# Products with the values in plain float32, two heads side by side, in a fused attention and MLP kernel

## The chip, the cores and the metric

The kernel runs on one core of one Trainium2 chip. The metric is the device time of one execution in microseconds (us). Three runs of the kernel before took 716.34, 716.54 and 716.68 us; the median is 716.54.

TensorE (PE in the profile; PEld is its loading of weights) multiplies matrices: a stationary operand of up to 128 rows by 128 columns is loaded, and a moving operand of up to 512 columns streams past it into a bank of PSUM. VectorE (DVE), ScalarE (ACT) and GpSimd (POOL) work element by element, and SyncE (SP) issues the transfers.

## The reference

Attention with a window and sinks, then a two-layer MLP with squared ReLU:

```python
scores = (1 / sqrt(64)) * q @ k.T            # q, k, v: 4 batches, 8 heads, 768 positions, 64 wide
keep = (key < n_sink) | (0 <= query - key < window)      # n_sink 4, window 128
a = exp(scores_kept - max);  a = a / (sum(a) + 1e-9)
x = a @ v                                     # then (3072 tokens, 512)
g = s * relu(x @ w_in) ** 2 + b               # w_in 512 x 2048
out = g @ w_out                               # w_out 2048 x 512
```

All of it is float32.

## The kernel before, in words

The 3072 tokens are eight chunks of 384 (`CH`), three blocks of 128 (`BLK`, `P`). `ORDER` gives the batch and the half of the sequence of each chunk: chunks one and two are the first halves of batches 0 and 1, three and four their second halves, five and six the halves of batch 2, seven and eight those of batch 3. So of chunks three to eight, four are second halves and two are first halves.

The main loop at the end of the kernel (lines 785 to 800) runs the MLP of chunk c step by step (`moe_steps`: 16 first-layer steps `l1` with twelve matmuls of 384 columns at L610, 16 second-layer steps `l2` with nine of 512 columns at L630), and after each step it issues the slots of the attention of chunk c+1 that are due by then. So matmuls of the attention stand between blocks of MLP matmuls in TensorE's order, which is the order in which the code issues them.

Attention of the first two chunks is the class `Plain` (L461 to L566), with products in plain float32; its product with the values is L555: for each block of keys and each of a pair's two heads, a stationary block of values of 64 columns, with the first head's result in partitions 0 to 63 of a bank and the second's in 64 to 127. Attention from the third chunk on is `attn_slots` (L418), which the change touches. There most products are made in `float32r`, a form of float32 of which TensorE takes a reduced precision in one instruction; to keep the precision, an operand is split into a high part (a copy to float32r) and a low part (what the copy left out).

`attn_slots` has one unit for each head h and block i of 128 queries, so six for a pair of heads, and one slot for each unit. A slot t runs, in this order: loads and preparations that are due (`ahead`), the products with the values of unit t-7 (`unit_c`, `LC` = 7), the scores of unit t (`unit_a`), the work on the transposed exponentials of unit t-4 (`unit_b`, `LB` = 4), the ends of a pair (`sinks`, `scaled`), and the transpose of unit t-3 (`turn`).

- `load_pair` (L244) loads a pair's queries and values, five slots ahead of its first unit; `load_keys` a head's keys, through one buffer; `prep_head` (L278) splits a head's queries, keys and values. The values become a stationary block of 128 columns, high part in 64 of them and low part in the others (L293 ACT, L294 POOL).
- `unit_a` (L297): two matmuls (L308, L309) for scores, a mask with maximum (L313), the exponential (L319), and POOL's additions and sink copies (L322, L323).
- `turn` (L329): the exponentials of 128 queries and 128 keys (those of two key blocks laid over one another) are transposed on TensorE.
- `unit_b` (L331): the two key blocks are separated by a multiplication with the masks `split` (L342 DVE, 256 columns), and the result is split into a high part (L344 ACT) and a low part (L345 POOL) in the tile `hl`, one for each head. The very first block of a sequence has one key block alone (L347, L348).
- `unit_c` (L360): at a head's block i=1 and at its block i=2, the products with the values. At i=1 high and low parts against the block of keys cur-1 (256 columns each, L382), and in second halves against one further block (128 columns each). At i=2 both parts of the last 128 columns in one matmul of 2 x 128 (L374), and two of 256 columns (L382). Each product has the high values' result in one half of the bank and the low values' in the other; L389 (ACT), L390 (DVE) and L392 (POOL) add them.
- `sinks` and `scaled` add the sinks' values (L406, L407) and divide by the sums (L413, L414), and L415 and L416 split the result for the MLP.

The planner that orders the instructions keeps this order on each engine, and each engine works through its own queue in order.

Of the kernel before, what the change touches and what calls it, by code (L numbers as in the profile page):

```python
# [6 lines left out]
F32 = mybir.dt.float32  # L7
F32R = mybir.dt.float32r
# [19 lines left out]
MDT = mybir.dt.bfloat16  # L28
WUP = 256.0
LOADS = 8  # L30
SMB, HLB = 4, 2
WARM0 = 14
NARROW, NEARLY = 2, 8
RB, VB = 1, 2
E0 = 16
PART = 256
FN, FB, FC = (3, 2), (7, 8), (11, 12)
# [4 lines left out]
def tile_kernel(ctx, tc, qT, kT, k0, v, vsk, n_sink, window, w, s, b, out):  # L42
# [201 lines left out]
    def load_pair(k, pr):  # L244

        pp = Chunk()
        k.pairs[pr] = pp
        half = k.half
        nkb, k0, kw, v0 = 3 + half, (0, 2 * P + 2 * NS)[half], (3 * P + 2 * NS, 4 * P + 2 * NS)[half], half * 2
        pp.q = wk.tile([P, CH], F32, name="qraw", tag="qraw", bufs=1)  # L250
        nc.sync.dma_start(pp.q, qT[k.b, pr, :, half * CH:(half + 1) * CH])
        pp.v = wk.tile([P, 4, 2, D], F32, name="vraw", tag="vraw", bufs=1)
        nc.sync.dma_start(pp.v[:, :nkb], v[k.b, pr, :, v0:v0 + nkb])
        for hh in range(2):
            hd = Chunk()
            hd.nkb, hd.kw, hd.k0, hd.half = nkb, kw, k0, slice(hh * D, (hh + 1) * D)
            hd.q, hd.v = pp.q[hd.half], pp.v[:, :, hh]
            k.heads[2 * pr + hh] = hd
        pp.psk = psks[(k.c * (H // 4) + pr // 2) % 2]
        pp.zz = wk.tile([P, BLK, 2], F32, tag="zz", name="zz", bufs=2)  # L260

    def load_keys(k, h):

# [14 lines left out]
    def prep_head(k, h):  # L278
        hd = k.heads[h]
        kw = hd.kw  # L280
        hd.qs = wk.tile([P, CH], F32R, tag="qs", name="qs")

        other = slice(D, 2 * D) if h % 2 == 0 else slice(0, D)
        nc.scalar.copy(hd.qs[hd.half], hd.q)  # L284
        hd.kh = wk.tile([P, 4 * P + 2 * NS], F32R, tag="kh", name="kh")
        hd.kl = wk.tile([P, 4 * P + 2 * NS], F32R, tag="kl", name="kl")
        nc.scalar.copy(hd.kh[:, :kw], hd.k[:, :kw])  # L287
        nc.vector.tensor_tensor(out=hd.qs[other], in0=hd.q, in1=hd.qs[hd.half].bitcast(F32), op=ALU.subtract)  # L288
        nc.gpsimd.tensor_tensor(out=hd.kl[:, :kw], in0=hd.k[:, :kw], in1=hd.kh[:, :kw].bitcast(F32), op=ALU.subtract)  # L289
        hd.vv = wk.tile([P, 4, P], F32R, tag="vv", name="vv", bufs=VB)  # L290
        a, c = (0, D) if h % 2 == 0 else (D, 0)
        n = hd.nkb
        nc.scalar.copy(hd.vv[:, :n, a:a + D], hd.v[:, :n, :])  # L293
        nc.gpsimd.tensor_tensor(out=hd.vv[:, :n, c:c + D], in0=hd.v[:, :n, :], in1=hd.vv[:, :n, a:a + D].bitcast(F32),  # L294
                                op=ALU.subtract)

    def unit_a(k, h, i, sc):  # L297

# [31 lines left out]

    def unit_b(k, h, i, tp):  # L331

        sm, c0, p0, _ = k.cc.pop((h, i))
        hd = k.heads[h]
        if i == 0:
            hd.hl = wk.tile([P, 2, 2 * CH], F32R, name="hl", tag="hl", bufs=HLB)

        a, z = (P if p0 is None else 0), 2 * P
        hi, lo = (hd.hl[:, t, i * z + a:(i + 1) * z] for t in range(2))
        if p0 is not None:  # L340
            both = wk.tile([P, 2 * P], F32, tag="two", name="two", bufs=2)
            nc.vector.tensor_tensor(out=both.rearrange("p (s c) -> p s c", s=2), in0=tp.unsqueeze(1).to_broadcast([P, 2, P]), in1=split,  # L342
                                    op=ALU.mult)
            nc.scalar.copy(hi, both)  # L344
            nc.gpsimd.tensor_tensor(out=lo, in0=both, in1=hi.bitcast(F32), op=ALU.subtract)  # L345
        else:
            nc.scalar.copy(hi, tp)  # L347
            nc.vector.tensor_tensor(out=lo, in0=tp, in1=hi.bitcast(F32), op=ALU.subtract)  # L348
        pp = k.pairs[h // 2]
        if h % 2 == 1 and i == BLK - 1:  # L350
            z0 = 12 * NS + h // 2 % 2 * 4
            zr = wk.tile([P, 2, BLK, 2], F32, tag="zr", name="zr")
            zh = wk.tile([P, BLK, 2], F32R, tag="zh", name="zh")
            nc.vector.tensor_scalar(out=zr[:, 0], in0=pp.zz, scalar1=1e-9, scalar2=None, op0=ALU.add)
            nc.vector.reciprocal(out=zr[:, 1], in_=zr[:, 0])
            nc.vector.tensor_copy(zh, zr[:, 1])
            nc.gpsimd.tensor_copy(out=pp.psk[:, :, z0:z0 + 2], in_=zh.bitcast(F32))
            nc.vector.tensor_tensor(out=pp.psk[:, :, z0 + 2:z0 + 4], in0=zr[:, 1], in1=zh.bitcast(F32), op=ALU.subtract)

    def unit_c(k, h, i):  # L360

        hd = k.heads[h]
        pp = k.pairs[h // 2]
        cur = i if k.half == 0 else i + 1
        if i == 1:
            hd.o = ps("o")
            hd.n = 0

        mm = []
        if i == BLK - 1:
            c0 = (2 * i + 1) * P
            nc.tensor.matmul(hd.o[:, i * P:], hd.vv[:, cur, :], hd.hl[:, :, c0:c0 + P], start=False, stop=False)  # L374
        if i > 0:
            mm.append((cur - 1, 2 * i - 1, 2))
        if i == 1 and k.half == 1:
            mm.append((0, 0, 1))
        for kb, c0, n in mm:
            for t in range(2):  # L380
                q0 = c0 // 2 * P
                nc.tensor.matmul(hd.o[:, q0:q0 + n * P], hd.vv[:, kb, :], hd.hl[:, t, c0 * P:(c0 + n) * P],  # L382
                                 start=(hd.n == 0), stop=(i == BLK - 1 and kb == cur - 1 and t == 1))
                hd.n += 1
        if i == BLK - 1:
            a, c = (0, D) if h % 2 == 0 else (D, 0)
            if h % 2 == 0:
                pp.x = wk.tile([P, CH + P], F32, tag="y", name="y", bufs=3)
            nc.scalar.copy(pp.x[a:a + D], hd.o[c:c + D])  # L389
            nc.vector.tensor_tensor(out=pp.x[a:a + D], in0=hd.o[a:a + D], in1=pp.x[a:a + D], op=ALU.add)  # L390
            if h % 2 == 1:
                nc.gpsimd.tensor_tensor(out=pp.x[:, CH - P:CH], in0=pp.x[:, CH - P:CH], in1=pp.x[:, CH:], op=ALU.add)  # L392
                pp.x = pp.x[:, :CH]
            if h % 4 == 3:
                ts = ps("ts")
                for j in range(BLK):
                    nc.tensor.transpose(ts[:, j * P:(j + 1) * P], pp.psk[:, j, :], ident)  # L397
                pp.xs = k.pairs[h // 2 - 1].xs = wk.tile([P, CH], F32R, tag="xsk", name="xsk", bufs=1)
                nc.scalar.copy(pp.xs, ts[:, :CH])
                nc.vector.tensor_tensor(out=pp.xs[32:64], in0=ts[32:64, :CH], in1=pp.xs[32:64].bitcast(F32), op=ALU.subtract)  # L400
# [17 lines left out]
    def attn_slots(c):  # L418
        k = new_chunk(c)
        units, ahead = [], {}  # L420
        for pr in range(H // 2):
            h, t0 = 2 * pr, 2 * BLK * pr
            units += [(h + hh, i) for hh in range(2) for i in range(BLK)]
            todo = ((-5, load_pair, pr), (-5, load_keys, h), (11, load_sinks, pr), (-2, prep_head, h), (-2, load_keys, h + 1),
                    (1, prep_head, h + 1))
            for d, fn, a in todo:
                ahead.setdefault(max(t0 + d, 0), []).append((fn, a))
        n = len(units)
        ends = {}
        for pr in range(H // 2):  # L430
            t = 4 * BLK * (pr // 2 + 1) - 1 + LC
            for d, fn in zip((LD if pr < H // 2 - 2 else LDL)[pr % 2], (sinks, scaled)):
                ends.setdefault(t + d, []).append((fn, pr))

        def slot(t):
            def f():

                for fn, a in ahead.get(t, ()):
                    fn(k, a)
                if t == 0:  # L440
                    k.bank = ps("sc")
                if 0 <= t - LC < n:
                    unit_c(k, *units[t - LC])
                if t < n:
                    unit_a(k, *units[t], k.bank)
                if 0 <= t - LB < n:
                    unit_b(k, *units[t - LB], k.bank[:, 3 * P:])
                for fn, pr in ends.get(t, ()):
                    fn(k, pr)
                if t + 1 < n + LB:  # L450
                    k.bank = ps("sc")
                if 0 <= t + 1 - LB < n:
                    turn(k, *units[t + 1 - LB], k.bank[:, 3 * P:])
            return f

        parts = [slot(t) for t in range(n + LC + LDL[1][1])]
        parts.pop(n + LB)
        return k, parts
# [391 lines left out]
```

## Time and profile before

One execution was profiled: it took 715.33 us, and its span from the first to the last instruction is 713.6 us.

| engine | busy us | share of the span | instructions |
|---|---|---|---|
| PE (matmuls) | 693.0 | 97% | 3908 |
| PEld (weight loads) | 613.8 | 86% | 3908 |
| DVE | 500.6 | 70% | 1186 |
| ACT | 469.4 | 66% | 1153 |
| POOL | 385.3 | 54% | 671 |

The mean granted clock of TensorE is 0.998 of its full speed. The main groups are L610 (1536 matmuls, 297.6 us) and L630 (1152 matmuls, 295.9 us), the MLP.

How to read it: a matmul's row gives its start and its length, and lengths of neighbours overlap, since they are pipelined; the distance from one start to the next is what a matmul adds to the time. In a group's row, the number behind the bar is the busy time, then the mean length of one in ns, then the idle time of the engine before them and what ended it. Shapes such as 128\*64 are rows by columns of the stationary block. A row of the timeline with a count behind it merges neighbours that are alike.

### The profile page before, as it was taken

Reading aid. Unit: us, or ns where it says so; the run is one execution under the profiler, and the core shown is the slowest. Engines: PE = TensorE matmul, PEld = TensorE weight load, DVE = VectorE, ACT = ScalarE, POOL = GpSimd, SP = SyncE. Lnnn points to the kernel's source line nnn. Section 1 sums busy time; section 2 is a strip of 40 time slices with the busy share of each in tenths; the row PEclk is TensorE's granted clock in tenths of the full one; section 3 lists DMA queues with packets and bytes.
Section 4 is the critical chain, followed back from the end, with each engine's and each line's share of the span. In section 5 each row is a group of like instructions: output and inputs, shape, how many; then the busy total and the mean of one; then the engine's idle time right before and its main releaser. Section 6 shows DMA issues by size and latency. Waiting matters only on the chain.

```text
span 713.6 us, 12060 instructions
## 1 busy us (share of the span) xinstructions
PE 693.0 (97%) x3908; PEld 613.8 (86%) x3908; DVE 500.6 (70%) x1186; ACT 469.4 (66%) x1153; POOL 385.3 (54%) x671
## 2 busy tenths in 40 slices
PE   8799999999999999999999999999999999999996
PEld 4477877899989998899999999899998999899895
DVE  6899979488865798657885788657786588743321
ACT  6999975578845786467764787556774677733222
POOL 2356635379843899336671788625773488700000
PEclk9999999999999999999999999999999999999999
DMA  7873140322112122021111121111221221000001
GB/s 283 355 269 130 34 155 27 108 66 57 57 56 75 42 81 55 17 82 58 50 57 65 51 72 51 35 64 53 57 63 37 80 66 42 1 30 15 1 1 49
DMA packets 27382, 52.63 MB, mean 74 GB/s; under 512 B 3504, under 2 KB 15536, under 8 KB 25392
## 3 DMA queue, kind: packets, MB, share of 16 engines
q1 hardware_dynamic: 27312, 51.79, 22.0%
q8 instruction: 33, 0.54, 0.3%
q14 instruction: 37, 0.30, 0.1%
HBM read 45.49 MB, written 6.29 MB: 73 GB/s over the span
## 4 chain that ended last, share of the span: by engine, by line
PE 76%; DVE 6%; ACT 3%; POOL 2%; issue 1%; DMA 1%; POOLq 0%; ACTq 0%; DVEq 0%
PE h L610 32%; PE po L630 32%; PE o L382 3%; PE sc L308 2%; PE sc L309 2%; PE sc L329 2%; DVE w L230 1%; DMA w<-in_w 1%; DVE w L220 1%; PE o L374 1%; DVE wt L219 1%; POOL hl L345 1%; POOL kl L289 1%; PE os L406 1%; PE ts L397 1%
## 5 line engine op out<-in xcount | busy, mean ns | idle before, releaser
L610 PE MATMUL h<-x,w 128*128 128x384 f32 x1536 | 297.6, 342 | 6.0 <-DVE w L230 2.6
L630 PE MATMUL po<-w,g 128*128 128x512 f32 x1152 | 295.9, 402 | 0.0
L610 PEld LDWEIGHTS h<-x,w 128*128 128x128 f32 x1536 | 264.8, 188 | 14.3 <-DVE w L230 3.3
L630 PEld LDWEIGHTS po<-w,g 128*128 128x128 f32 x1152 | 209.8, 189 | 43.7 <-issue 1.6
L616 DVE SCALAR_TENSOR_TENSOR r<-h,sb,r 128x384 f32<-128x384 f32 x112 | 68.9, 615 | 78.8 <-ACT r L613 77.9
L613 ACT ACTIVATE r<-h 128x384 f32<-128x384 f32 x128 | 62.9, 491 | 90.6 <-PE h L610 81.1
L619 DVE SCALAR_TENSOR_TENSOR g<-r,sb,g 128x384 fp32r<-128x384 f32 x112 | 91.5, 817 | 31.3 <-ACT g L618 29.7
L345 POOL TENSOR_TENSOR hl<-two,hl 128x256 fp32r<-128x256 f32 x128 | 102.3, 801 | 15.4 <-ACT hl L344 13.3
L322 POOL TENSOR_TENSOR sm<-sm 128x128 f32<-128x128 f32 x128 | 67.4, 527 | 61.2 <-ACT sm L319 59.0
L319 ACT ACTIVATE sm<-sm,negm 128x264 f32<-128x264 f32 (+1 forms) x144 | 72.1, 500 | 28.5 <-DVE negm L313 27.3
L618 ACT ACTIVATE g<-r,sb 128x384 fp32r<-128x384 f32 x112 | 69.1, 617 | 22.7 <-DVE r L616 21.9
L206 POOL TENSOR_TENSOR w<-w 128x256 int32<-128x256 int32 x60 | 48.6, 840 | 54.3 <-DVE zf L532 15.1
L289 POOL TENSOR_TENSOR kl<-kraw,kh 128x528 fp32r<-128x528 f32 (+1 forms) x48 | 60.8, 1266 | 20.7 <-ACT kh L287 20.4
L344 ACT CAST hl<-two 128x256 fp32r<-128x256 f32 x128 | 50.5, 394 | 26.0 <-DVE two L342 25.7
L342 DVE TENSOR_TENSOR two<-sc,split 128x256 f32<-128x256 f32 x128 | 53.1, 417 | 5.8 <-POOL hl L345 5.5
L323 POOL COPY psk<-sm 128x24 f32<-128x24 f32 x144 | 35.5, 247 | 17.1 <-ACT sm L319 17.0
L382 PE MATMUL o<-hl,vv 128*128 128x256 f32 (+1 forms) x256 | 44.3, 275 | 0.0
L382 PEld LDWEIGHTS o<-hl,vv 128*128 128x128 f32 x256 | 39.6, 188 | 3.2
L288 DVE TENSOR_TENSOR qs<-qraw,qs 64x384 fp32r<-64x384 f32 x48 | 39.7, 827 | 3.5 <-ACT qs L284 1.9
L313 DVE CUSTOM_DVE_ANT_0 sm<-sc,msk 128x264 f32<-128x264 f32 (+1 forms) x80 | 32.0, 400 | 14.0 <-PE sc L309 13.4
L308 PE MATMUL sc<-kh,qs 128*128 128x264 f32 (+1 forms) x144 | 41.6, 291 | 0.0
L313 DVE CUSTOM_DVE_ANT_0 sm<-sc,m_all 128x264 f32<-128x264 f32 x64 | 27.3, 426 | 20.1 <-PE sc L309 18.4
(139 smaller groups left out, 924.0 us busy)
## 6 DMA issues: line engine op xcount, KB each, us to landing
w<-in_w SPq DMA_DIRECT2D x15, 1024.0 KB, 10.5
kraw<-in_kT SPq DMA_DIRECT2D x32, 264.0 KB, 2.6
out<-ot SPq DMA_DIRECT2D x24, 256.0 KB, 2.0
qraw<-in_qT SPq DMA_DIRECT2D x24, 192.0 KB, 2.4
vraw<-in_v SPq DMA_DIRECT2D x16, 256.0 KB, 2.7
kraw<-in_kT SPq DMA_DIRECT2D x16, 200.0 KB, 2.4
vsraw<-in_vsk SPq DMA_DIRECT2D x24, 64.0 KB, 2.1
vraw<-in_v SPq DMA_DIRECT2D x8, 192.0 KB, 2.4
```

Of the source, the lines that this page charges most:

```text
L289: nc.gpsimd.tensor_tensor(out=hd.kl[:, :kw], in0=hd.k[:, :kw], in1=hd.kh[:, :kw].bitcast(F32), op=ALU.subtract)
L313: nc.vector.tensor_tensor_reduce(out=sm[:, :n], in0=sc[:, :n], in1=m, scale=-0.125, scalar=BIG, op0=ALU.add, op1=ALU.min, accum_out=negm[: ...
L319: nc.scalar.activation(sm[:, :n], sm[:, :n], AF.Exp, bias=negm[:, uu], scale=-1.0, accum_out=pp.zz[:, i, hh:hh + 1])
L322: nc.gpsimd.tensor_tensor(out=sm[:, c1:c1 + P], in0=sm[:, p1:p1 + P], in1=sm[:, c1:c1 + P], op=ALU.add)
L345: nc.gpsimd.tensor_tensor(out=lo, in0=both, in1=hi.bitcast(F32), op=ALU.subtract)
L382: nc.tensor.matmul(hd.o[:, q0:q0 + n * P], hd.vv[:, kb, :], hd.hl[:, t, c0 * P:(c0 + n) * P], start=(hd.n == 0), stop=(i == BLK - 1 and kb ...
L610: nc.tensor.matmul(h[:, :CH], weight[f][:, 0, wi, cc * P:(cc + 1) * P], x[xi][:, cc, :], start=(i == 0), stop=(i == 11))
L613: nc.scalar.activation(r, h[:, :CH], AF.Relu, scale=1.0 / WUP)
L616: nc.vector.scalar_tensor_tensor(out=hr, in0=h[:, :CH], scalar=sw_ap, in1=r, op0=ALU.mult, op1=ALU.mult)
L618: nc.scalar.activation(gg[:, 0, :], hr, AF.Identity, bias=b_ap, scale=1.0)
L619: nc.vector.scalar_tensor_tensor(out=gg[:, 1, :], in0=hr, scalar=b_ap, in1=gg[:, 0, :].bitcast(F32), op0=ALU.add, op1=ALU.subtract)
L630: nc.tensor.matmul(po[tb], gg[:, gi, tsl], weight[f][:, 1, wi, :], start=(f == 0 and i == 0), stop=(f == NF - 1 and i == 2))
```

## The change

From the third chunk on the values stay as they are loaded, and are no longer split: `load_values` loads a pair's values into a tile of the ring `vv`, five slots behind the pair's first unit (`VL` = 5), not with the queries five slots ahead of it. The transposed exponentials stay whole as well: L342 writes them into a tile `pp.t` for the two heads of a pair (the ring `hl`, the same size), and L344, L345 and L348 go. The products of both heads are made at the units i=1 and i=2 of the pair's second head, in plain float32: stationary 64 columns of values, the first head's result in partitions 0 to 63 and the second's in 64 to 127, in one bank for the pair. So the sum of parts (L390, L392) goes, and one copy of 128 x 384 is left of L389.

```diff
-SMB, HLB = 4, 2
+SMB, HLB, VL = 4, 2, 5
...
-RB, VB = 1, 2
+RB = 1
...
 def load_pair(k, pr):
...
-        pp.v = wk.tile([P, 4, 2, D], F32, name="vraw", tag="vraw", bufs=1)
-        nc.sync.dma_start(pp.v[:, :nkb], v[k.b, pr, :, v0:v0 + nkb])
+        pp.v0, pp.nkb = v0, nkb
...
+    def load_values(k, pr):
+        pp = k.pairs[pr]
+        pp.v = wk.tile([P, 4, 2, D], F32, name="v", tag="vv", bufs=2)
+        nc.sync.dma_start(pp.v[:, :pp.nkb], v[k.b, pr, :, pp.v0:pp.v0 + pp.nkb])
...
 def prep_head(k, h):
...
-        hd.vv = wk.tile([P, 4, P], F32R, tag="vv", name="vv", bufs=VB)
-        a, c = (0, D) if h % 2 == 0 else (D, 0)
-        n = hd.nkb
-        nc.scalar.copy(hd.vv[:, :n, a:a + D], hd.v[:, :n, :])
-        nc.gpsimd.tensor_tensor(out=hd.vv[:, :n, c:c + D], in0=hd.v[:, :n, :], in1=hd.vv[:, :n, a:a + D].bitcast(F32),
-                                op=ALU.subtract)
...
 def unit_b(k, h, i, tp):
-        sm, c0, p0, _ = k.cc.pop((h, i))
-        hd = k.heads[h]
-        if i == 0:
-            hd.hl = wk.tile([P, 2, 2 * CH], F32R, name="hl", tag="hl", bufs=HLB)
-
-        a, z = (P if p0 is None else 0), 2 * P
-        hi, lo = (hd.hl[:, t, i * z + a:(i + 1) * z] for t in range(2))
+        _, _, p0, _ = k.cc.pop((h, i))
+        pp = k.pairs[h // 2]
+        if h % 2 == 0 and i == 0:
+            pp.t = wk.tile([P, 2, 2 * CH], F32, name="tt", tag="hl", bufs=HLB)
+        z = 2 * P
+        both = pp.t[:, h % 2, i * z:(i + 1) * z]
         if p0 is not None:
-            both = wk.tile([P, 2 * P], F32, tag="two", name="two", bufs=2)
             nc.vector.tensor_tensor(out=both.rearrange("p (s c) -> p s c", s=2), in0=tp.unsqueeze(1).to_broadcast([P, 2, P]), in1=split,
                                     op=ALU.mult)
-            nc.scalar.copy(hi, both)
-            nc.gpsimd.tensor_tensor(out=lo, in0=both, in1=hi.bitcast(F32), op=ALU.subtract)
         else:
-            nc.scalar.copy(hi, tp)
-            nc.vector.tensor_tensor(out=lo, in0=tp, in1=hi.bitcast(F32), op=ALU.subtract)
-        pp = k.pairs[h // 2]
+            nc.scalar.copy(both[:, P:], tp)
...
 def unit_c(k, h, i):
-        hd = k.heads[h]
         pp = k.pairs[h // 2]
         cur = i if k.half == 0 else i + 1
+        if h % 2 == 0 or i == 0:
+            return
         if i == 1:
-            hd.o = ps("o")
-            hd.n = 0
-        mm = []
-        if i == BLK - 1:
-            c0 = (2 * i + 1) * P
-            nc.tensor.matmul(hd.o[:, i * P:], hd.vv[:, cur, :], hd.hl[:, :, c0:c0 + P], start=False, stop=False)
-        if i > 0:
-            mm.append((cur - 1, 2 * i - 1, 2))
+            pp.o = ps("o")
+        mm = [(cur - 1, 2 * i - 1, 2)]
         if i == 1 and k.half == 1:
             mm.append((0, 0, 1))
+        if i == BLK - 1:
+            mm.insert(0, (cur, 2 * i + 1, 1))
         for kb, c0, n in mm:
-            for t in range(2):
-                q0 = c0 // 2 * P
-                nc.tensor.matmul(hd.o[:, q0:q0 + n * P], hd.vv[:, kb, :], hd.hl[:, t, c0 * P:(c0 + n) * P],
-                                 start=(hd.n == 0), stop=(i == BLK - 1 and kb == cur - 1 and t == 1))
-                hd.n += 1
+            q0 = c0 // 2 * P
+            for hh in range(2):
+                nc.tensor.matmul(pp.o[hh * D:(hh + 1) * D, q0:q0 + n * P], pp.v[:, kb, hh], pp.t[:, hh, c0 * P:(c0 + n) * P],
+                                 start=(i == 1 and kb == cur - 1), stop=(i == BLK - 1 and kb == cur - 1))
         if i == BLK - 1:
-            a, c = (0, D) if h % 2 == 0 else (D, 0)
-            if h % 2 == 0:
-                pp.x = wk.tile([P, CH + P], F32, tag="y", name="y", bufs=3)
-            nc.scalar.copy(pp.x[a:a + D], hd.o[c:c + D])
-            nc.vector.tensor_tensor(out=pp.x[a:a + D], in0=hd.o[a:a + D], in1=pp.x[a:a + D], op=ALU.add)
-            if h % 2 == 1:
-                nc.gpsimd.tensor_tensor(out=pp.x[:, CH - P:CH], in0=pp.x[:, CH - P:CH], in1=pp.x[:, CH:], op=ALU.add)
-                pp.x = pp.x[:, :CH]
+            pp.x = wk.tile([P, CH], F32, tag="y", name="y", bufs=3)
+            nc.scalar.copy(pp.x, pp.o[:, :CH])
...
-            todo = (..., (-2, load_keys, h + 1), (1, prep_head, h + 1))
+            todo = (..., (-2, load_keys, h + 1), (VL, load_values, pr), (1, prep_head, h + 1))
```

## Rows read from the trace of the kernel before

**Rows 1.** The page's busy times: us, share of the span, instructions.
```profile
PE 693.0 (97%) x3908; PEld 613.8 (86%) x3908; DVE 500.6 (70%) x1186; ACT 469.4 (66%) x1153; POOL 385.3 (54%) x671
```

**Rows 2.** Table of stretches: length, then PE, PEld, DVE, ACT, POOL, clock, DMA.
```profile
142.00:642.00 500.00, 497.83 (x2802) 456.11 (x2801) 365.32 (x874) 336.03 (x876) 320.91 (x575) 1.00 0.18 54
```

**Rows 3.** Waits of PE from 140 to 640 us: total, times, longest.
```profile
PE h L610 <- DVE y L414: 1.9, 3, 1.1
```

**Rows 4.** Groups by line and shape, PE: count, busy us, mean ns, idle.
```profile
L382 PE MATMUL o<-hl,vv 128*128 128x256 f32 x192 | 38.8, 283 | 0.0
...
L382 PE MATMUL o<-hl,vv 128*128 128x128 f32 x64 | 10.8, 249 | 0.0
...
L555 PE MATMUL o<-tf,vf 128*64 128x256 f32 x16 | 2.4, 379 | 0.0
```

**Rows 5.** Timeline of PE, values visit in chunk two: start, length, line, count.
```profile
75.67 0.40 PE L630 MATMUL po<-w,g 128*128 128x512 f32 x1
76.00 0.54 PE L555 MATMUL o<-tf,vf 128*64 128x384 f32 x2
76.37 0.49 PE L555 MATMUL o<-tf,vf 128*64 128x384 f32 x2
76.70 0.39 PE L555 MATMUL o<-tf,vf 128*64 128x256 f32 x2
76.91 0.39 PE L555 MATMUL o<-tf,vf 128*64 128x256 f32 x2
77.13 0.39 PE L555 MATMUL o<-tf,vf 128*64 128x128 f32 x4
77.35 0.28 PE L560 MATMUL zb<-identr,zf 128*64 128x128 f32 x2
...
77.89 0.28 PE L560 MATMUL zb<-identr,zf 128*64 128x128 f32 x2
78.10 0.45 PE L610 MATMUL h<-x,w 128*128 128x384 f32 x1
78.38 0.34 PE L610 MATMUL h<-x,w 128*128 128x384 f32 x1
```

**Rows 6.** Timeline of PE around three values visits of later chunks.
```profile
238.56 0.40 PE L630 MATMUL po<-w,g 128*128 128x512 f32 x1
238.79 0.57 PE L382 MATMUL o<-hl,vv 128*128 128x256 f32 x4
239.20 0.33 PE L308 MATMUL sc<-kh,qs 128*128 128x264 f32 x1
239.37 0.28 PE L309 MATMUL sc<-kl,qs 128*128 128x264 f32 x1
...
241.55 0.34 PE L610 MATMUL h<-x,w 128*128 128x384 f32 x1
241.73 0.28 PE L374 MATMUL o<-hl,vv 128*128 128x256 f32 x1
...
242.08 0.28 PE L308 MATMUL sc<-kh,qs 128*128 128x264 f32 x1
242.21 0.29 PE L309 MATMUL sc<-kl,qs 128*128 128x264 f32 x1
...
324.01 0.40 PE L382 MATMUL o<-hl,vv 128*128 128x256 f32 x2
324.25 0.28 PE L308 MATMUL sc<-kh,qs 128*128 128x264 f32 x1
```

**Rows 7.** POOL's L345; DVE's timeline before L414; the load of values.
```profile
L345 POOL TENSOR_TENSOR hl<-two,hl 128x256 fp32r<-128x256 f32 x128 | 102.3, 801 | 15.4 <-ACT hl L344 13.3
...
197.69 0.42 DVE L342 TENSOR_TENSOR two<-sc,split 128x256 f32<-128x256 f32 x1 [1.74 <-POOL hl L345]
...
199.74 0.56 DVE L414 TENSOR_TENSOR y<-zb,y 128x384 f32<-128x384 f32 x1
...
vraw<-in_v SPq DMA_DIRECT2D x16, 256.0 KB, 2.7
```

More of the change, by code (lines that the diff above doesn't have):

```diff
@@ L256, in load_pair @@
             hd.nkb, hd.kw, hd.k0, hd.half = nkb, kw, k0, slice(hh * D, (hh + 1) * D)
-            hd.q, hd.v = pp.q[hd.half], pp.v[:, :, hh]
+            hd.q = pp.q[hd.half]
             k.heads[2 * pr + hh] = hd
@@ L423, in attn_slots @@
             units += [(h + hh, i) for hh in range(2) for i in range(BLK)]
-            todo = ((-5, load_pair, pr), (-5, load_keys, h), (11, load_sinks, pr), (-2, prep_head, h), (-2, load_keys, h + 1),
+            todo = ((-5, load_pair, pr), (-5, load_keys, h), (11, load_sinks, pr), (-2, prep_head, h), (-2, load_keys, h + 1), (VL, load_values, pr),
                     (1, prep_head, h + 1))
```

## The prediction, made before the change was run

> **What bounds the kernel now.** I read the page's busy shares first, and the reader is to see that TensorE (PE) is at 97% and no other engine over 70% [rows 1]. A share over the whole span can hide stages, so next comes the table of stretches for 142 to 642 us, in which all the attention work of chunks three to eight lies: PE is busy 497.83 of 500.00 us there, VectorE (DVE) 365, ScalarE (ACT) 336, GpSimd (POOL) 321 [rows 2]. PE's idle time is thus 500.00 - 497.83 = 2.2 us, and the list of waits gives 1.9 us of it to one cause, L610 waiting for the DVE multiply L414, three times [rows 3]. So in the stage that changes, time is what PE's own instructions take, one start after another, and whatever the change takes off the other three engines can pay 2.2 us at most.
>
> A busy PE row doesn't give that time: a matmul's row holds its way through the array too, and rows overlap. What counts is the distance from one start to the next. For a 512-column L630 this is 238.79 - 238.56 = 0.23 us, for a 384-column L610 241.73 - 241.55 = 0.18 [rows 6], though their rows last 0.40 and 0.34.
>
> **The products before.** A head's value products come in two visits to PE, its block i=1 and its block i=2. For the chunks of the second half of a sequence (four of the six: 16 pairs of heads) the first visit has two matmuls of 256 columns and two of 128: 239.20 - 238.79 = 0.41 us, and the L308 behind takes 239.37 - 239.20 = 0.17 until L309 starts, where it takes 242.21 - 242.08 = 0.13 behind a visit that ends on 256 columns; I count the 0.04 to the visit: 0.45. The second visit, L374 and two L382, takes 242.08 - 241.73 = 0.35. For the two chunks of the first half (8 pairs) the first visit has 256 columns twice, 324.25 - 324.01 = 0.24 [rows 6]. The counts agree. 192 L382 of 256 columns are four for each of 48 heads, 64 of 128 two for each of 32 [rows 4]. Sum: 32 heads x (0.45 + 0.35) + 16 x (0.24 + 0.35) = 25.6 + 9.4 = 35.0 us.
>
> **The products after.** The trace has their like: L555 in the two first chunks is a plain float32 product, 64 weight columns, one head over the other in one bank, looped over the heads in the same way. Each call is two PE instructions (16 for the 8 calls of 256 columns in one chunk [rows 4]). A step, both heads at one block of keys, so four instructions, is two pairs of starts: for 256 columns 76.91 - 76.70 = 0.21 and 77.13 - 76.91 = 0.22, together 0.43; for 128 columns 77.35 - 77.13 = 0.22 together [rows 5]. These contain whatever the two heads do beside each other. A pair's i=1 visit is now one step of 256 columns and, in the second half, one of 128: 0.43 or 0.65; its i=2 visit is one of each, 0.65. Sum of the streams: 16 x 1.30 + 8 x 1.08 = 29.4 us, 5.6 less than before.
>
> **What the change adds: going into and out of the 64-column form.** In front of L555 the L630 takes 76.00 - 75.67 = 0.33 instead of 0.23: +0.10. The first pair of 384 columns takes 76.37 - 76.00 = 0.37, the second 76.70 - 76.37 = 0.33: +0.04 (its weights are loaded with nothing running beside them). The last pair before a 128-column matmul takes 78.10 - 77.89 = 0.21 instead of 0.11: +0.10. The first L610 behind takes 78.38 - 78.10 = 0.28 instead of 0.18: +0.10 [rows 5, 6]. Together 0.34 us a visit. In the first two chunks this is paid once a pair; from the third on it is paid at each visit, since each visit stands between matmuls of MLP and scores (before, L630 or L610 ahead and L308 behind [rows 6]). There are 24 pairs x 2 = 48 visits: 48 x 0.34 = 16.3 us. The trace has no such step with L308 or a transpose behind it, so I bound the price. From below: only the 0.10 on going in and 0.04 for the first weights, if leaving were hidden by the short L308, 0.14 or 6.7 us. From above: the full 0.34 and another 0.10, if L309's weights are late as well, 0.44 or 21.1 us. I take 0.34, the row whose neighbours (L610, L630) stand in front of most visits.
>
> At this place the Trainium skill bears on weight loads: "TensorE: Matmul & The Clock Gate", Part 3, The mechanism, says that a weight load runs under running matmuls only where it uses other rows of the array. All products here use all 128 rows, so by that rule the weights of every pair of starts would be exposed as in the first pair. The trace disagrees within a visit: the second pair of 384 columns takes 0.33 and those of 256 take 0.21 to 0.22, as their columns would at one rate, and only the first pair has the 0.04 [rows 5].
>
> **What goes from the other engines.** Copies and subtractions for the low parts: L345 alone was 102.3 us of POOL [rows 7], with L344 (ACT), L293 and L294 (values), half of L389 and all of L390 and L392 beside it. All of this stood beside a PE that was busy with MLP matmuls, so I cost it at nothing but for PE's 2.2 us of idle time. Of that, the 1.9 us behind L414 should go. At the longest of the three, L414 starts at 199.74 in a DVE queue that had stood still for 1.74 us at L342, waiting for POOL's L345 [rows 7]; that wait goes with L345. Next late there would be L390's and the normalizers' work ahead of L414 in the same queue, and L390 goes too. I take -1.6 us, since one of the three may stay (bounds 0 and -2.2). The load of the values is moved from five slots ahead of a pair to five slots behind its begin. In SP's queue it now stands behind this pair's second keys and the next pair's queries and two keys, and the last of these waits until POOL's L289 has freed the one key buffer, some slot earlier; nothing behind it in that queue gets later than by its own issue, and its old place is freed for the loads that waited behind it. From its new place to its first use are six slots; a slot is some 241.73 - 238.79 = 2.9 us and a values load lands in 2.7 us [rows 6, 7], so 17 us cover 2.7 and a slot of waiting. POOL's and ACT's split of the values (L294, L293) isn't moved but gone. If that cover were gone, PE would wait up to 2.7 us in each of 24 pairs. A pair's exponentials are kept until the odd head's visits; the ring of two lasts, since a pair is freed before the pair after the next begins to write.
>
> **Sum.** -5.6 + 16.3 - 1.6 = +9.1 us. The profiled execution took 715.33 us (span 713.6 and 1.7 around it); that gives 724.4. The median of the runs is 716.54, 1.2 above, so for the time measured I say 725.6 us.
>
> **Rivals.**
> (a) Leaving and entering is hidden, so that only the streams count: 716.5 - 5.6 - 2.2 = 708.7 us, faster. This decides from a price under (5.6 + 1.6) / 48 = 0.15 us a visit on. For it: the streams are shorter, and L308 and L309 are short. Against: 0.34 at the visit of rows 5, on both sides, with both L630 and L610 as neighbours. 5 in 100; in between, at a price of 0.14 to 0.18, no change that can be measured: 5.
> (b) The two heads' products don't run beside each other as in L555, because an order of instructions sets them apart: each step takes twice as long, 725.6 + 29.4 = 755 us. Against: the same loop over heads as L555. 3.
> (c) Weights exposed at every pair of starts as they are at the first: 16 x 8 + 8 x 6 = 176 pairs less the 48 first ones, 128 x 0.04 = 5.1 us: 730.7 us. It could still happen where the pair before is short (128 columns, 0.11). 6. (This is what the rule of the page on the clock gate in the Trainium skill would make of it.)
> (d) A new wait: values or exponentials late at the odd head's visit, 24 x 0.5 = 12 us: 737.6. Against: six slots of cover. 4.
> The forecast itself: 77.
>
> **How the numbers follow.** With the price of a visit between 0.20 and 0.42, and the relief between 0 and 2.2, the forecast runs from 716.5 - 5.6 + 9.6 - 2.2 = 718.3 to 716.5 - 5.6 + 20.2 = 731.1; ends that need both extremes are cut a little: 719.5 to 731. That holds (c) and leaves (a), (b) and (d) out. A measurement here tells some 0.2% (1.4 us) from no change. Slower by more: the forecast, (b), (c), (d): 0.90. Within: 0.05. Faster by more: 0.05.
>
> **What would show it.** In the trace after: L382's and L374's 128-column rows gone, products in pairs of starts 0.21 apart at 256 columns and 0.11 at 128; a stretched matmul ahead of each visit (0.33 for L630), 0.21 for its last pair, and L308 at 0.2 or more behind it; PE busy as before, idle near none in the attention stretch, POOL less busy by at least L345's 102 us; the waits L610 for L414 and L342 for L345 gone. I am wrong if matmuls at the edges of a visit keep their usual distance, or if L555's pairs are not found again, or if PE has a new wait for v or the exponentials.

## The result, and the profile after

The changed kernel takes 722.51 us (median of four runs, 720.96 to 723.65) where the kernel before took 716.44 beside it: a ratio of 1.0083, 95% interval 1.0064 to 1.0102, so slower by some 6 us. 725.6 had been forecast, in a range from 719.5 to 731. The profiled execution took 722.75 us, its span is 720.6.

The page's busy times and, from the table of stretches, the same 500 us as in [rows 2] (length, then PE, PEld, DVE, ACT, POOL, granted clock, DMA share, GB/s):

```profile
PE 703.6 (98%) x3956; PEld 595.7 (83%) x3956; DVE 461.4 (64%) x1122; ACT 400.0 (56%) x953; POOL 246.2 (34%) x471
...
142.00:642.00 500.00, 500.00 (x2823) 431.77 (x2822) 325.31 (x807) 264.68 (x675) 183.21 (x378) 1.00 0.18 53
```

GpSimd is 139 us less busy than in [rows 1], ScalarE 69, VectorE 39, and the time went up: TensorE, which had 2.2 us without a row in that stretch [rows 2], now has none, and its wait of [rows 3] is gone. The products are there in the form of L555 [rows 4], 64 columns, 352 instructions for 304 (by line and shape):

```profile
L369 PE MATMUL o<-tt,v 128*64 128x256 f32 x192 | 30.1, 392 | 0.0
...
L369 PE MATMUL o<-tt,v 128*64 128x128 f32 x160 | 16.8, 288 | 0.0
```

One visit at a block i=1 of a second half, on TensorE's timeline (start, length, line, shape, count; a row merges neighbours, so that of 262.29 holds the pair of 256 columns there and the next pair):

```profile
261.70 0.40 PE L610 MATMUL po<-w,g 128*128 128x512 f32 x1
262.02 0.44 PE L369 MATMUL o<-tt,v 128*64 128x256 f32 x2
262.29 0.49 PE L369 MATMUL o<-tt,v 128*64 128x256 f32 x4
262.51 0.39 PE L369 MATMUL o<-tt,v 128*64 128x128 f32 x4
262.62 0.28 PE L369 MATMUL o<-tt,v 128*64 128x128 f32 x2
262.83 0.39 PE L307 MATMUL sc<-kh,qs 128*128 128x264 f32 x1
263.05 0.28 PE L308 MATMUL sc<-kl,qs 128*128 128x264 f32 x1
263.18 0.27 PE L328 MATMUL sc<-identr,sm 128*128 128x128 f32 x1
```

Read the starts. The last MLP matmul (L610 here is the L630 of before) takes 0.32 to the next start instead of 0.23; the first pair 0.27 where the second takes 0.22; a pair of 128 columns 0.11, and the last one 0.21; L307 behind it 0.22, where the same step takes 0.13 without an edge [rows 6] (L307, L308 and L328 here are the L308, L309 and L329 of before, L590 is L610 and L596 is L616). These are the four extras of [rows 5], now at each visit, L307 included, which the trace of before could not show.

To weigh the attention alone I take, in each run, the time from the first first-layer matmul of the second chunk's MLP to that of the eighth's; all attention of chunks three to eight lies between. Before, 639.28 - 133.18 = 506.10; after, 646.68 - 134.76 = 511.92, so +5.82 us, where the forecast's sum was +9.1 (rows of both timelines, before first):

```profile
133.18 0.34 PE L610 MATMUL h<-x,w 128*128 128x384 f32 x1
...
639.28 0.34 PE L610 MATMUL h<-x,w 128*128 128x384 f32 x1
```

```profile
134.76 0.34 PE L590 MATMUL h<-x,w 128*128 128x384 f32 x1
...
646.68 0.34 PE L590 MATMUL h<-x,w 128*128 128x384 f32 x1
```

The other 1.58 us of this profile are there at 134.76 already, and come from the start, where both kernels issue the same matmuls. From 24 to 26 us TensorE was at half its clock (table of stretches):

```profile
20.00:37.00 17.00, 12.62 (x93) 7.53 (x91) 14.55 (x36) 16.24 (x39) 6.52 (x8) 0.90 0.79 317
...
24.00:26.00 2.00, 2.00 (x10) 0.91 (x8) 1.33 (x3) 2.00 (x3) 1.35 (x3) 0.50 1.02 426
```

### The profile page after: what moved, and what is told of

It is laid out like the page before. It is cut to its first block, busy times and chain, and to the rows that moved or that the text cites. A ratio compares the mean times of both kernels' runs of the same rounds, so it can differ in the third digit from the quotient of the medians.

```text
span 720.6 us, 11671 instructions
## 1 busy us (share of the span) xinstructions
PE 703.6 (98%) x3956; PEld 595.7 (83%) x3956; DVE 461.4 (64%) x1122; ACT 400.0 (56%) x953; POOL 246.2 (34%) x471
## 4 chain that ended last, share of the span: by engine, by line
PE 83%; DVE 3%; DMA 1%; ACT 1%; issue 0%; POOL 0%
PE po L610 34%; PE h L590 33%; PE o L369 5%; PE sc L307 3%; PE sc L308 2%; PE sc L328 2%; PE ts L377 1%; DMA w<-in_w 1%; DVE w L230 1%; PE os L386 1%; PE zb L393 1%; DVE w L220 1%; DVE wt L219 1%; POOL w L206 0%; DVE g L599 0%
## 5 line engine op out<-in xcount | busy, mean ns | idle before, releaser
L590 PE MATMUL h<-x,w 128*128 128x384 f32 x1536 | 298.0, 342 | 4.1 <-DVE w L230 2.6
L610 PE MATMUL po<-w,g 128*128 128x512 f32 x1152 | 295.8, 402 | 0.0
L590 PEld LDWEIGHTS h<-x,w 128*128 128x128 f32 x1536 | 264.8, 188 | 13.6 <-DVE w L230 3.3
L610 PEld LDWEIGHTS po<-w,g 128*128 128x128 f32 x1152 | 210.0, 188 | 43.8 <-issue 1.6
L596 DVE SCALAR_TENSOR_TENSOR r<-h,sb,r 128x384 f32<-128x384 f32 x112 | 68.9, 615 | 80.8 <-ACT r L593 80.1
L321 POOL TENSOR_TENSOR sm<-sm 128x128 f32<-128x128 f32 x128 | 68.9, 538 | 149.3 <-ACT sm L318 139.0
L599 DVE SCALAR_TENSOR_TENSOR g<-r,sb,g 128x384 fp32r<-128x384 f32 x112 | 94.0, 839 | 39.6 <-ACT g L598 37.8
L396 POOL TENSOR_TENSOR x<-y,x 128x384 fp32r<-128x384 f32 x18 | 18.5, 1029 | 106.6 <-ACT x L395 106.6
L339 DVE TENSOR_TENSOR tt<-sc,split 128x256 f32<-128x256 f32 x128 | 52.8, 416 | 0.2
L322 POOL COPY psk<-sm 128x24 f32<-128x24 f32 x144 | 34.0, 236 | 27.7 <-ACT sm L318 27.7
L307 PE MATMUL sc<-kh,qs 128*128 128x264 f32 (+1 forms) x144 | 42.8, 299 | 0.0
L308 PE MATMUL sc<-kl,qs 128*128 128x264 f32 (+1 forms) x144 | 40.9, 285 | 0.0
L369 PE MATMUL o<-tt,v 128*64 128x256 f32 (+1 forms) x352 | 40.1, 344 | 0.0
L328 PE MATMUL sc<-identr,sm 128*128 128x128 f32 x144 | 39.4, 274 | 0.0
```

What stands on the lines that cost most here:

```text
L307: nc.tensor.matmul(sc[:, :n], hd.qs[:, qs], hd.kh[:, c0:c0 + n], start=True, stop=False)
L321: nc.gpsimd.tensor_tensor(out=sm[:, c1:c1 + P], in0=sm[:, p1:p1 + P], in1=sm[:, c1:c1 + P], op=ALU.add)
L369: nc.tensor.matmul(pp.o[hh * D:(hh + 1) * D, q0:q0 + n * P], pp.v[:, kb, hh], pp.t[:, hh, c0 * P:(c0 + n) * P], start=(i == 1 and kb == cu ...
L590: nc.tensor.matmul(h[:, :CH], weight[f][:, 0, wi, cc * P:(cc + 1) * P], x[xi][:, cc, :], start=(i == 0), stop=(i == 11))
L596: nc.vector.scalar_tensor_tensor(out=hr, in0=h[:, :CH], scalar=sw_ap, in1=r, op0=ALU.mult, op1=ALU.mult)
L599: nc.vector.scalar_tensor_tensor(out=gg[:, 1, :], in0=hr, scalar=b_ap, in1=gg[:, 0, :].bitcast(F32), op0=ALU.add, op1=ALU.subtract)
```

## The experiments

The stretch from chunk two to chunk eight in each run, worked out in the same way from the start of every 192nd first-layer matmul, and the time of the runs:

| run | visits | second-half chunks, us | first-half chunks, us | six chunks, us | median, us | ratio to before, 95% |
|---|---|---|---|---|---|---|
| before | - | 86.21, 85.33, 85.33, 84.67 | 82.29, 82.29 | 506.10 | 715.6 to 716.4 | 1 |
| after | 48 | 85.72, 85.71, 85.71, 85.71 | 84.54, 84.54 | 511.92 | 722.51 | 1.0064 to 1.0102 |
| after, again | 48 | 85.72, 85.71, 85.71, 85.71 | 84.54, 84.54 | 511.92 | 721.74 | 1.0072 to 1.0098 |
| one visit for a pair | 24 | 84.33, 84.31, 84.31, 84.31 | 83.09, 83.09 | 503.46 | 713.35 | 0.9957 to 0.9981 |
| one visit for four heads | 12 | 83.76, 83.75, 83.75, 83.75 | 82.81, 82.84 | 500.66 | 710.57 | 0.9922 to 0.9946 |
| visits split | 72 | 87.26, 87.24, 87.24, 87.24 | 85.09, 85.09 | 519.16 | 730.26 | 1.0186 to 1.0212 |
| 128 columns | 0 | 88.67, 88.64, 88.64, 88.63 | 86.42, 86.41 | 527.41 | 737.65 | 1.0293 to 1.0322 |
| before, no low parts | - | 84.74, 84.76, 84.76, 84.73 | 82.40, 82.42 | 503.81 | 713.66 | 0.9962 to 0.9981 |
| before, no low parts, no sum | - | 84.78, 84.74, 84.76, 84.76 | 82.40, 82.41 | 503.85 | 713.52 | 0.9957 to 0.9981 |
| after, two banks | 48 | 85.69, 85.68, 85.68, 85.68 | 84.49, 84.49 | 511.72 | 721.75 | 1.0067 to 1.0094 |
| before, wait filled | - | 85.79, 85.12, 85.11, 84.64 | 82.29, 82.29 | 505.24 | 715.82 (one run) | - |

**The changed kernel again.** No edit.

> The changed kernel once more. In its profile the attention stretch (from the first MLP step to the last one) is 5.8 us longer than before, but its first MLP matmul already starts 1.5 us later, after a stretch at half clock from 23.8 to 27.2 us that the kernel before does not have, although both issue the same TensorE work up to there. Theory: this start is a matter of the execution and not of the change; then it comes and goes from run to run, and runs without it lie near 721 us (716.4 + 5.8 - 0.4 at the end, less what the clock rose late). Rival: the change makes the start slower; then all runs have it, and none is under 722.

Five runs gave 721.09 to 721.97, and the profiled one has no stretch at half clock at the start; its MLP of chunk two begins at 132.93, 0.25 us ahead of before:

```profile
20.00:37.00 17.00, 12.65 (x102) 8.27 (x103) 15.57 (x37) 17.00 (x37) 6.56 (x8) 1.00 0.78 312
...
132.93 0.34 PE L590 MATMUL h<-x,w 128*128 128x384 f32 x1
```

The attention stretch is 511.92 once more. The mean clock was 0.995 to 0.999 from run to run in the kernel before as well, with times from 714.5 to 717.2 us on this chip. So the late start is no part of the change, its rival fell, and the change itself is worth the 5.8 us of the stretch.

**One visit for a pair.**

```diff
-        if h % 2 == 0 or i == 0:
+        if h % 2 == 0 or i < BLK - 1:
             return
-        if i == 1:
-            pp.o = ps("o")
...
+        pp.o = ps("o")
+        mm = [(cur - 2, 1, 2)] + ([(0, 0, 1)] if k.half == 1 else []) + [(cur, 5, 1), (cur - 1, 3, 2)]
...
```

> The changed kernel with both visits of a pair made one: all products with the values of a pair are issued together at block i=2 of its second head, so 24 visits to the 64-column form and not 48, with the same products. Theory (each way in and out costs 0.35 us): 24 x 0.35 = 8.4 us less than the changed kernel, near 713 to 714, below the kernel before. Rival (the cost lies in the plain float32 products themselves, however they are grouped): no change, 721 to 723.

713.35 us: 8.4 less than the changed kernel beside it, and faster than before. In the stretch, 511.92 - 503.46 = 8.46 us for 24 visits saved, 0.35 each, with the same products. The rival fell. A visit is now one row of sixteen instructions, with 0.33 us ahead of it (192.33 - 192.00):

```profile
192.00 0.40 PE L605 MATMUL po<-w,g 128*128 128x512 f32 x1
...
192.33 1.52 PE L364 MATMUL o<-tt,v 128*64 128x256 f32 x16
```

**Visits split.** The two products of a visit are set on either side of the score matmuls of their slot.

```diff
...
-        for kb, c0, n in mm:
+        for kb, c0, n in mm[part:part + 1]:
...
-                    unit_c(k, *units[t - LC])
+                    unit_c(k, *units[t - LC], 0)
                 if t < n:
                     unit_a(k, *units[t], k.bank)
+                if 0 <= t - LC < n:
+                    unit_c(k, *units[t - LC], 1)
```

> The changed kernel with the two products of a visit set apart by the two score matmuls of the same slot, where the slot has any: 24 more ways into and out of the 64-column form (five in each of the four second-half chunks, two in each of the two first-half chunks), the same products. Theory (0.35 us each): +8.4 us, 722 + 8.4, near 730. Rival (what was won by one visit came from fewer stops of another kind, such as PE waiting for exponentials at the first visit): 722.

730.26 us, as expected; in the stretch 519.16 - 511.92 = 7.24 us for 24 visits more, 0.30 each. On the timeline the two products and the scores between them, with the edge at each turn (163.73 - 163.51 = 0.22 for L307, 163.95 - 163.73 = 0.22 for L308, which is 0.13 without one):

```profile
163.14 0.44 PE L369 MATMUL o<-tt,v 128*64 128x128 f32 x4
163.51 0.39 PE L307 MATMUL sc<-kh,qs 128*128 128x264 f32 x1
163.73 0.28 PE L308 MATMUL sc<-kl,qs 128*128 128x264 f32 x1
163.95 0.65 PE L369 MATMUL o<-tt,v 128*64 128x256 f32 x4
```

**128 columns.** Both heads' values are one stationary block, and each head has its own bank.

```diff
-            pp.o = ps("o")
+            pp.o = [ps("o") for _ in range(2)]
...
-                nc.tensor.matmul(pp.o[hh * D:(hh + 1) * D, q0:q0 + n * P], pp.v[:, kb, hh], pp.t[...],
+                nc.tensor.matmul(pp.o[hh][:, q0:q0 + n * P], pp.v[:, kb].rearrange("p h d -> p (h d)"), pp.t[...],
...
-            nc.scalar.copy(pp.x, pp.o[:, :CH])
+            for hh in range(2):
+                nc.scalar.copy(pp.x[hh * D:(hh + 1) * D], pp.o[hh][hh * D:(hh + 1) * D, :CH])
```

> The changed kernel with a stationary block of all 128 columns (both heads' values) for each head, each head's result in a bank of its own; the half of each result that belongs to the other head is not used. No 64-column form any more, still plain float32. Theory (the edges are paid for the change between 128 and 64 columns, and two heads in 64 columns each run beside each other): streams double, +29.4 us, edges go, -16.8: +12.6, near 735 us, and matmuls at the edges of a visit keep their usual distance. Rival 1 (edges are paid for plain float32 beside float32r): +29.4, near 751. Rival 2 (the two heads did not run beside each other): -16.8, near 705.

737.65 us; the stretch is 15.5 us longer than after, where the doubled streams alone would be 29.4, so the edges gave back 13.9 of the 16.8 expected, 0.29 a visit. The matmul ahead of the visit keeps its distance (175.95 - 175.71 = 0.24), and instructions start one by one, 0.21 apart (176.16 - 175.95), not in pairs:

```profile
175.71 0.40 PE L611 MATMUL po<-w,g 128*128 128x512 f32 x1
175.95 0.59 PE L369 MATMUL o<-tt,v 128*128 128x256 f32 x2
...
176.16 0.59 PE L369 MATMUL o<-tt,v 128*128 128x256 f32 x2
...
176.81 0.61 PE L369 MATMUL o<-tt,v 128*128 128x128 f32 x4
177.17 0.37 PE L307 MATMUL sc<-kh,qs 128*128 128x264 f32 x1
177.38 0.28 PE L308 MATMUL sc<-kl,qs 128*128 128x264 f32 x1
```

L307's 0.21 isn't an edge that is left. The last product starts 0.03 ahead of L307 (four starts 0.11 apart from 176.81 on), so L307's row holds that product's time: from 176.81 to L308 it is 0.57, which is 4 x 0.11 + 0.13, four products and an L307 without an edge. So the edge belongs to the change between 128 and 64 columns and not to plain float32; and the two heads do run beside each other in the 64-column form. Both rivals fell. Why the edges gave back 0.29 a visit and not 0.35 wasn't settled.

**Before, without the low parts.**

```diff
-            nc.gpsimd.tensor_tensor(out=lo, in0=both, in1=hi.bitcast(F32), op=ALU.subtract)
...
-            nc.vector.tensor_tensor(out=lo, in0=tp, in1=hi.bitcast(F32), op=ALU.subtract)
...
-                nc.tensor.matmul(hd.o[:, q0:q0 + n * P], hd.vv[:, kb, :], hd.hl[:, t, c0 * P:(c0 + n) * P],
+                nc.tensor.matmul(hd.o[:, q0:q0 + n * P], hd.vv[:, kb, :], hd.hl[:, 0, c0 * P:(c0 + n) * P],
```

> The kernel before without the low parts of the exponentials: L345 on GpSimd (102 us) and L348 on VectorE are left out, and the second product of each block takes the high part again in place of the low one. TensorE's instructions are the same. Theory (the other engines' relief pays only what TensorE waited): its waits for L414 (1.9 us) and for the transposes L329 in second halves (three of 0.23, one of 0.17) go, some 2 to 3 us: 713.5 to 714.5. Rival 1 (TensorE is the bound and the relief is worth nothing): 716.4. Rival 2 (the chain behind the exponentials holds more than the profile's idle time): 710 or less.

713.66 us, and the stretch is 506.10 - 503.81 = 2.29 us shorter. The time is the expected one, but partly by luck. The list of waits no longer has L414, and it now has the transposes that were expected to stop waiting:

```profile
PE sc L329 <- DVE r L614: 1.1, 4, 0.3
```

By the starts, L414's waits were worth more than the 1.9 us of the list. In the kernel before, the next L610 starts 1.45, 0.72 and 0.71 us behind the L329 ahead of it, where it takes 0.03 when nothing waits, so 2.8 us in all. The first of the three:

```profile
198.90 0.33 PE L329 MATMUL sc<-identr,sm 128*128 128x128 f32 x1
...
200.35 0.44 PE L610 MATMUL h<-x,w 128*128 128x384 f32 x1 [1.12 <-DVE y L414]
```

These went, and the waits of the transposes grew.

**After, with a second bank for a pair.**

```diff
+        if h % 2 == 0 and i == 1:
+            pp.d = ps("o")
+            nc.vector.memset(pp.d[:, 0:1], 0.0)
+        if h % 2 == 0 and i == BLK - 1:
+            nc.scalar.copy(dump, pp.d[:, 0:1])
```

> The changed kernel, in which the first head of each pair takes a bank of PSUM again at its block i=1 and gives it back at its block i=2, as before the change; one column is written and one read there, no TensorE instruction is added. Part of what the change saved beyond the waits for L414 are waits of the transposes L329 in second halves (L309 to L329 0.36 us in place of 0.12), where the bank for the next scores is not yet free. Theory (the change's saved bank took these waits away): they come back, 0.3 to 0.5 us in each second-half chunk, +1 to +2 us, near 723. Rival (VectorE's relief took them away): no wait comes back, the same time as the changed kernel, 721.7.

721.75 us and 511.72 in the stretch: no wait came back. The theory of the saved bank fell.

**Before, without low parts and without the sum.** The edits of the run without low parts, and these:

```diff
...
-            nc.scalar.copy(pp.x[a:a + D], hd.o[c:c + D])
-            nc.vector.tensor_tensor(out=pp.x[a:a + D], in0=hd.o[a:a + D], in1=pp.x[a:a + D], op=ALU.add)
+            nc.scalar.copy(pp.x[a:a + D], hd.o[a:a + D])
...
-                nc.gpsimd.tensor_tensor(out=pp.x[:, CH - P:CH], in0=pp.x[:, CH - P:CH], in1=pp.x[:, CH:], op=ALU.add)
```

> The kernel before without the low parts of the exponentials (as in the run without them) and without the sum of the two halves of a bank: L390 on VectorE (33 us) and L392 on GpSimd (11 us) are left out, and the copy L389 takes the high values' half alone. TensorE's instructions and the banks are as before. Theory of the saved bank: TensorE still waits for L329 in second halves, the attention stretch takes what it took without the low parts alone (503.8 us from the first MLP step of chunk two to that of chunk eight), 713.5 us. Rival (VectorE's relief): these four waits of 0.43 us go, 502.1 us in the stretch, 712 us.

713.52 us and 503.85 in the stretch: the four waits stay, each at 0.43 us, so VectorE's relief isn't it either. Two more of 0.18 us stand in the first-half chunks, which are 0.11 us longer than before; the list of PEld, the weight loads, has all six:

```profile
PEld sc L329 <- issue: 2.7, 6, 0.5
```

The timeline at one of the four:

```profile
274.93 0.28 PE L309 MATMUL sc<-kl,qs 128*128 128x264 f32 x1
275.49 0.30 PE L329 MATMUL sc<-identr,sm 128*128 128x128 f32 x1 [0.27 <-DVE r L612]
```

L329 starts 0.56 us behind L309, 0.43 more than the 0.13 from L308 to L328 in the visit of the changed kernel above. The row's mark gives 0.27 of it; the rest lies under the end of L309's row. L612 is the MLP's L616, which reads the bank of the first layer's result. So TensorE waits for a bank that L616 frees. That gave a third theory: the bank comes free at a fixed time after the MLP matmuls, and in the changed kernel the wait isn't removed but filled, by the longer visit that stands ahead of it.

**Before, with the wait filled.**

```diff
+            if k.half == 1 and h == 5 and i == 1 and n == 2:
+                for _ in range(2):
+                    nc.tensor.matmul(hd.o[:, :2 * P], hd.vv[:, kb, :], hd.hl[:, 0, P:3 * P], start=True, stop=True)
             for t in range(2):
```

> The kernel before with two matmuls of 256 columns more (0.12 us each by their starts) in the values visit that stands just ahead of the waiting transpose L329, once in each second-half chunk (the sixth head's block i=1); each writes the same first product once more and is overwritten. Theory (the longer visits of the changed kernel fill a wait that TensorE had there anyway, since the bank for L329's slot comes free at a fixed time after the MLP's L610): the distance from L309 to L329 falls from 0.36 to some 0.12, and a second-half chunk takes no longer: 84.67 us for the last of them, 506.1 for the stretch of six. Rival (the wait moves along with the work): the distance stays at 0.36 and each second-half chunk is 0.24 longer, 84.9 and 507.0.

The last second-half chunk takes 84.64 us with two matmuls more, against 84.67 without; the other three are even shorter (85.79, 85.12, 85.11 for 86.21, 85.33, 85.33), as L414's waits fell from 1.9 to 1.0 us in PE's list. The distance from L309 to L329, before and here:

```profile
276.83 0.28 PE L309 MATMUL sc<-kl,qs 128*128 128x264 f32 x1
277.19 0.33 PE L329 MATMUL sc<-identr,sm 128*128 128x128 f32 x1
```

```profile
277.77 0.28 PE L309 MATMUL sc<-kl,qs 128*128 128x264 f32 x1
277.89 0.33 PE L329 MATMUL sc<-identr,sm 128*128 128x128 f32 x1
```

0.36 became 0.12: 0.24 us of TensorE work cost nothing at this place. The rival fell.

That the changed kernel fills this wait in the same way, and that no relief of ScalarE or GpSimd took it away, is read from the same place of both traces, before first:

```profile
275.73 0.28 PE L308 MATMUL sc<-kh,qs 128*128 128x264 f32 x1
276.52 0.61 DVE L616 SCALAR_TENSOR_TENSOR r<-h,sb,r 128x384 f32<-128x384 f32 x1
```

```profile
276.62 0.28 PE L307 MATMUL sc<-kh,qs 128*128 128x264 f32 x1
277.52 0.61 DVE L596 SCALAR_TENSOR_TENSOR r<-h,sb,r 128x384 f32<-128x384 f32 x1
278.38 0.27 PE L328 MATMUL sc<-identr,sm 128*128 128x128 f32 x1
```

From the first score matmul behind the MLP's first layer to the end of L616 it is 276.52 + 0.61 - 275.73 = 1.40 us before, and 277.52 + 0.61 - 276.62 = 1.51 after: counted from there, the bank comes free no earlier. The transpose starts 277.19 - 275.73 = 1.46 us behind that score matmul before, just after the bank is free, and 278.38 - 276.62 = 1.76 after, when it has been free for 0.25. In the run with a second bank, which takes its banks as before, these are 1.52 and 1.76.

**One visit for four heads.** The version that these point to: the products of two pairs together, five slots behind the scores, where the transposes and ends stay at seven.

```diff
+    def products(k, h, i):
+        if h % 4 < 3 or i < BLK - 1:
+            return
+        cur = i if k.half == 0 else i + 1
+        two = [k.pairs[h // 2 - 1], k.pairs[h // 2]]
...
+                if 0 <= t - LP < n:
+                    products(k, *units[t - LP])
...
```

> One visit for two pairs: all products with the values of four heads are issued together, two slots earlier after the last head's work than before (five slots behind the scores, so that the rings of two keep their size), 12 visits in place of 48; the transposes and ends keep their slots, and the sinks' load comes one slot earlier. Theory: 12 x 0.35 = 4.2 us less than with 24 visits, 713.4 - 4.2, near 709. Rival: the last head's exponentials come too late for the earlier visit and TensorE waits, up to a slot's part of 1 us at 12 visits: 713 to 721.

710.57 us, ratio 0.9934: the fastest of all. No wait for the last head's exponentials appeared ahead of a visit, and a visit is 32 instructions, some 2.75 us (203.62 - 200.87):

```profile
200.54 0.40 PE L613 MATMUL po<-w,g 128*128 128x512 f32 x1
200.87 2.82 PE L365 MATMUL o<-tt,v 128*64 128x256 f32 x32
203.62 0.45 PE L593 MATMUL h<-x,w 128*128 128x384 f32 x1
```

Against 24 visits the stretch is 2.80 us shorter, 0.23 for each of 12 and not 0.35 (0.28 in second halves, 0.14 in first halves). What first halves lack is a new wait, once in each of the two chunks: the MLP's first layer waits for the copy of the transposed exponentials of a sequence's first block (L342), which PEld's list shows and which isn't in that of the run with 24 visits. By the starts (358.92 - 358.62 = 0.30 instead of 0.03) it costs some 0.27 us for two visits, the 0.14 a visit that is missing:

```profile
PEld h L593 <- ACT tt L342: 0.7, 2, 0.4
...
358.62 0.27 PE L328 MATMUL sc<-identr,sm 128*128 128x128 f32 x1
358.92 0.45 PE L593 MATMUL h<-x,w 128*128 128x384 f32 x1
```

The rest, 0.28 and not 0.35, wasn't settled; the visits that went had other neighbours (L372's transposes, the sinks' L381) than those that stayed.

## Why the prediction was right, and where it was off

The forecast was slower by 9.1 us, for TensorE's edges; it came out slower, for the edges, by 5.8 us in the stretch and some 6 us in the runs. The direction and the mechanism were right. Of the 3.3 us between, 0.5 lies in the edges and streams, and 2.8 in the waits that went from TensorE, a term that was forecast too small.

- **TensorE is the bound:** right. 139 us taken from GpSimd bought nothing beyond TensorE's own waits, and what each kernel took followed TensorE's starts.
- **Streams, edges, and their sum (-5.6 + 16.3 = +10.7):** about right. The edge was forecast at 0.34 from a single visit to L555; halving the visits gave 0.35, splitting them 0.30. TensorE's work, freed of waits, grew by 511.92 - 503.85 + 4 x 0.43 + 2 x 0.18 = 10.2 us (after, against the kernel before without low parts and sum, whose six waits are taken out; with the four of second halves alone it is 9.8). Streams and edges can't be told apart within this sum to better than the spread of the edge price.
- **The wait for L414:** right that L345 held it; without the low parts it is gone. It was worth 2.8 us by the starts, and not the 1.9 of the list.
- **What goes from the other engines (-1.6, at most -2.2):** this is the term that was mis-sized. The relief alone is worth 2.3 us (no low parts), and 4 x 0.43 + 2 x 0.18 = 2.1 us more are waits that stay when the other engines are relieved and that TensorE's new work filled, so that this much of it cost nothing; the forecast had no such term. Together that is -4.4, and 10.2 - 4.4 = +5.8. (That this sum closes is no check of its own, since the same stretches are in each term. The trace before says the same by itself: its distances between starts, against the same steps where nothing waits, are longer by 2.8 us for L414, 0.9 at the transposes of second halves and some 0.7 in smaller pieces.) The bound of 2.2 came from PE's busy time, and a busy row covers a wait that is shorter than the row's tail: the transposes of second halves waited up to 0.36 - 0.12 = 0.24 us before, and PE's list of waits [rows 3] didn't have them. The list of PEld, which the prediction didn't use, has both, 4.1 us together:

```profile
PEld h L610 <- DVE y L414: 2.5, 3, 1.3
PEld sc L329 <- DVE r L616: 1.6, 6, 0.3
```

- **The rivals:** hidden edges (708.7) fell by the visits of the trace and by both runs that changed their number. Heads not beside each other fell by the 128-column run. Weights exposed at every pair fell by the starts: 0.27 for the first pair only, then 0.22 and 0.11. That was the rule in the Trainium skill, "TensorE: Matmul & The Clock Gate", Part 3, The mechanism; this kernel's rows don't show it within a visit. A new wait for values or exponentials ahead of the visits didn't come, not even with the products two slots earlier.

## What to carry to other kernels

Where TensorE is busy without a gap, count starts, not lengths, and price each change between full-width and half-width matmuls (0.3 us here): the products themselves were cheaper in the new form, and 48 small visits ate the gain, while 24 or 12 visits kept it. Don't look for the gain of a relieved engine beyond the waits of the bound one, and look for those waits in the distances between starts and in the list of the weight loads, not in the idle time of the matmul rows alone. Work added ahead of a wait with a fixed end was free as far as it was tried, 0.24 us here.

## What the runs showed that was not expected

The start of the kernel, where TensorE waits for inputs, differs from one execution to the next. Seven of the eleven profiles have a stretch at the lower of the two clocks that begins between 22 and 32 us; four have none, among them the kernel before and the repeat of the changed one. In the changed kernel's first profile TensorE had been busy for 0.19 of 2.00 us just ahead of it:

```profile
20.00:22.00 2.00, 0.19 (x4) 0.00 (x0) 1.75 (x6) 2.00 (x10) 0.00 (x0) 1.00 1.02 426
```

The kernel before was as idle there (0.21 of 2.00) and kept its clock. The first matmul of chunk one's MLP starts at 36.5 to 37.7 us in the seven, and at 35.8 to 36.2 in the four. So two executions can differ by up to 2 us there, a third of the effect that was studied; a stretch that begins behind it, as that of the table, doesn't contain it.
